# Row maxima split on VectorE before the turn, in an attention kernel that TensorE and VectorE share

## The chip, the cores and the metric

The kernel runs on one core of a Trainium2 chip. The metric is the device time of one execution in microseconds (us); of several runs the median counts. A profiled execution has a trace beside its time, and all durations below come from that one execution.

## The reference

Two branches with adaptive layer norm, one after the other, on `x` of 2048 rows by 512 columns: attention with 32 heads of 16 columns that share one key and one value head, and a bilinear gated feed-forward part with 1792 columns inside.

```
mod = (silu(c) @ w_mod).reshape(6, D)          # sa, ca, ga, sb, cb, gb
h = layernorm(x) * (1 + ca) + sa
q, k, v = h @ wq (32 heads x 16), h @ wk (16), h @ wv (16)
p = softmax(q k^T / 4)                         # per head, over 2048 keys
x = x + ga * ((p v) @ wo)
h = layernorm(x) * (1 + cb) + sb
x = x + gb * (((h @ w_gate) * (h @ w_up)) @ w_down)
```

## The kernel before

**Units.** The queries are cut into 4 blocks of 512 rows (`NB`), the 32 heads into 8 groups of 4 (`UB`); a block and a group make one of 32 units. Within a unit the keys go by in 16 tiles of 128 (`KT`). One step of the loop over key tiles is called a turn here: it makes four score products `sc` (L631, one for each head of the group, 128 keys by 512 queries), four exponentials on ScalarE (L633), and the four products `pv` of the turn before with the values (L642). So a unit has 16 turns, and `attend` writes two of them out at a time.

**Row maxima.** The exponentials need each query row's maximum over all keys, and it has to be there before a unit begins. Another set of score products `mx` (L581, 128 queries by 512 keys) therefore runs some 30 steps ahead, four in each turn; VectorE reduces each to one column of `mpart` (L584). When a unit's last `mx` has been reduced, `max_fin` (L601) takes the maximum over the four key blocks: `mm`, 128 rows by 16 columns. The maxima must then become rows of the operand `sst` of the next unit's score products: 48 of its 64 rows in each half hold the queries in f16 pieces, rows 48 and 49 (112 and 113 in the other half) the maximum, divided by 32, as a high and a low f16 part, so that the score product subtracts it by itself. `max_rows` does this. Its `f` turns `mm` on TensorE into a PSUM bank, `mxt` (L608). Its `g` writes the high part with a ScalarE copy (L613), the low part with a VectorE instruction that subtracts the high one (L614), both from PSUM into tiles `mt`, and sends each to `sst` with a DMA (L618) from SyncE's queue (SP).

**PSUM.** The eight banks (`NBANK`) are handed out from a queue: `ps_hold` takes the bank at its head, `ps_give` puts one back at its end, `ps_mx` and `ps_sc` do both at once. A TensorE product into a bank waits until the bank's last reader has finished. `pv` holds a bank for a whole unit, a side group holds one until it has ended.

**Side work.** Between the score products stand halves of side groups (L499): the q projection of later heads at first, then output projection and FFN of the block before. Each half uses 64 of TensorE's 128 rows, and a score product on the other 64 stands beside it. Three orders of a turn are written out by hand, `e` for a score product with its exponential, `m` for a maximum product, `x` for a half of a side group, the digit for the half of the rows:

```
NO_SIDE = "e0 e1 m0 m1 e0 e1 m0 m1"
FEW = "e1 m0 e0 x1 m0 x1 e0 x1 m0 x1 e1 m0"
MANY = "x1 e0 x1 m0 x1 e0 x1 e0 x1 m0 x1 m0 x1 m0 x1 e0"
```

FEW is for the q projection, MANY for output projection and FFN, NO_SIDE where no group is ready. In FEW and MANY the halves change roles in the second turn of each pair (`a ^ turn`).

**Order around the change.** `max_half` notes `f` and `g` in `later` when a unit's last maximum product has been issued, under the count of maximum steps from which they may run. `late_max` runs such an `f` and puts `g` into `posts`. It is called in the middle of a turn and behind the turn's `pv` products; `drain_posts` runs what is in `posts` at the start and in the middle of each turn, ahead of that half's products. `hooks` puts weight loads and other small steps between. With MANY and FEW two or more maximum products of the same half follow each other, and `f` comes to stand behind `pv` of the same turn in which the unit's last maximum product was made, `g` at the start of the next. The unit's last maximum product lies in its predecessor's turn 13 (counted from 0) with MANY and FEW, and at the end of turn 12 with NO_SIDE, where `f` then stands in the middle of turn 13. The new unit's first score products stand at the head of what would be turn 16.

Of the kernel before, what the change touches and what calls it, by code (L numbers as in the profile page):

```python
# [14 lines left out]
F16 = mybir.dt.float16  # L15
AF = mybir.ActivationFunctionType
OP = mybir.AluOpType
# [13 lines left out]
SPLIT_GAP = 2.5  # L31
NBANK = 8
QPRE = (20, 24)
TR_WAIT = 11
NHF = 12
V_STEP = 24
# [17 lines left out]
def adaln_mqa_glu_kernel(ctx: ExitStack, tc: tile.TileContext, x_in, wq_in, wk_in, wv_in, wo_in,  # L54
                         wg_in, wu_in, wd_in, c_in, wm_in, out):
    nc = tc.nc
# [5 lines left out]
    work = ctx.enter_context(tc.tile_pool(name="work", bufs=2))  # L62
# [7 lines left out]
    def ps_hold(name="side", shape=(128, 512)):  # L70

        tag, bufs = pool.popleft()
        t = psum.tile(list(shape), F32, name=name, tag=tag, bufs=bufs)
        held[id(t)] = (t, tag, bufs)
        return t

    def ps_give(t):
        _, tag, bufs = held.pop(id(t))
        pool.append((tag, bufs))
# [47 lines left out]
    ident = consts.tile([128, 128], F32, name="ident")  # L127
# [15 lines left out]
    identh = consts.tile([128, 128], F16, name="identh")  # L143
# [146 lines left out]
    for k in range(KC):  # L290
        for j in range(4):
            nc.tensor.matmul(pmA[32 * j:32 * j + 32, 0:256], silr[:, k, 0:32], wmA[:, k, 256 * j:256 * j + 256],
                             start=(k == 0), stop=(k == KC - 1))
# [248 lines left out]
    def load_q(u):  # L542
        b, g = divmod(u, UB)
        d = qd[b, g // 2].rearrange("(h e) l n -> e h l n", e=16)
        s = sst[u % 3]
        h0 = 4 * (g % 2)
        for a in range(2):
            for r, hl in ((0, 0), (1, 0), (2, 1)):
                nc.sync.dma_start(s[64 * a + 16 * r:64 * a + 16 * r + 16, :, :], d[:, h0 + a:h0 + a + 3:2, hl, :])
# [20 lines left out]
    def max_parts(u):  # L570
        if u < NU and u not in mparts:
            mparts[u] = work.tile([128, 2, 2, 4, 4], F32, name="mpart")
            if u == 0:
                nc.gpsimd.memset(mparts[u], LOW)

    def max_mm(u, a, op):
        kind, p, t, kc = op
        s = sst[u % 3]
        m = ps_sc() if kind == "diff" else ps_mx()
        keys = kdt[64 * a:64 * a + 48, :] if kind == "diff" else kst[64 * a:64 * a + 48, kc * 512:(kc + 1) * 512]  # L580
        nc.tensor.matmul(m, s[64 * a:64 * a + 48, p, t * 128:(t + 1) * 128], keys, start=True, stop=True)  # L581
        part = mparts[u][:, a, p, t, kc:kc + 1]
        if kind == "one":
            nc.vector.tensor_reduce(part, m, axis=AX.X, op=OP.max)  # L584
        elif kind == "diff":
            r = rel[a] = work.tile([128, 512], F32, name="rel", tag="gf", bufs=4)
            relus.append(lambda: nc.scalar.activation(r, m, AF.Relu))
        else:
            nc.vector.tensor_tensor_reduce(out=rel[a], in0=m, in1=rel[a], scale=1.0, scalar=LOW, op0=OP.add,
                                           op1=OP.max, accum_out=part)  # L590
# [6 lines left out]
    mms = {}  # L597
# [3 lines left out]
        nc.vector.tensor_reduce(mms[u], mparts[u].rearrange("p a q t k -> p a (q t) k"), axis=AX.X, op=OP.max)  # L601

    def max_rows(u):
        def f():
            mms[u, "b"] = ps_hold("mxt")
            p = mms[u, "b"][0:16, 0:128]
            mms[u, "p"] = p
            nc.tensor.transpose(p, mms[u].rearrange("p a c -> p (a c)"), ident)  # L608

        def g():  # L610
            p = mms[u, "p"]
            mt = [work.tile([16, 128], F16, name=f"mt{hl}") for hl in range(2)]
            nc.scalar.activation(mt[0], p, AF.Copy, scale=1.0 / 32.0)  # L613
            nc.vector.scalar_tensor_tensor(mt[1], p, 1.0 / 32.0, mt[0], op0=OP.mult, op1=OP.subtract)  # L614
            ps_give(mms[u, "b"])
            s = sst[u % 3]
            for hl in range(2):
                nc.sync.dma_start(s[48 + hl:113 + hl:64, :, :], mt[hl])  # L618
        return [(100, f, g)]

    pvb = {}
    ptl = {}
# [65 lines left out]
    def after(delay, f):  # L688
        if tick[0] is None:
            f()  # L690
        else:
            timers.setdefault(tick[0] + delay, []).append(f)
# [12 lines left out]
    def wo_work(b):  # L705
# [12 lines left out]
        def fin(t):  # L718
            def f(p):
# [28 lines left out]
                if t == 3:  # L748
                    for j, d in enumerate((2, 4, 6, 9) if b else (2, 4, 7, 12)):
                        after(d, n2f[b, j])  # L750
                    if b < NB - 1:
                        after(TR_WAIT if b else TR_WAIT + 3, lambda: turns.extend(ln2_work(b)))
            return f
# [7 lines left out]
    def ln2_work(b):  # L761
        items = []
        st = {}

        def tr(k):
            def f():
                if k == 0:
                    h2s[b] = big.tile([128, 2, KC, BT], F16, name="h2T", tag="wq")
                st["p"] = ps_hold("mx")
                for t in range(4):  # L770
                    nc.tensor.transpose(st["p"][:, t * 128:(t + 1) * 128], n2s[b, t][:, k * 128:(k + 1) * 128],  # L771
                                        ident)
            return f

        def ev(k):
            def f():
                hf = work.tile([128, BT], F32, name="hf", tag="g", bufs=2)
                nc.scalar.activation(hf, st["p"], AF.Identity, bias=hsc[:, k, 0:1], scale=hsc[:, k, 1:2])
                ps_give(st["p"])
                eng = nc.vector if b == NB - 1 else nc.gpsimd  # L780
                eng.tensor_scalar(h2s[b][:, 0, k, :], hf, 1.0, 0.0, op0=OP.mult, op1=OP.add)
                eng.tensor_tensor(h2s[b][:, 1, k, :], hf, h2s[b][:, 0, k, :], op=OP.subtract)
                if k == KC - 1:
                    h2done.add(b)
            return f

        for k in range(KC):
            items.append((900, tr(k), ev(k)))
        return items
# [248 lines left out]

    wlist, dlist, mod_rows = late_weights()
    NSTEP = 32  # L1040
    later = {}
    mstep = [0, 0]

    def drain_posts():
# [8 lines left out]
    def max_half(a):  # L1053
        n = mstep[a]
        mstep[a] += 1
        if n >= len(flat):
            return
        u, i, last, ops = flat[n]
        max_parts(u)
        for op in ops[a]:  # L1060
            max_mm(u, a, op)
        if a == 0:
            return
        if u + 1 < NU and i == QPRE[u > 0]:
            load_q(u + 1)
        if i == 12:
            max_parts(u + 1)
        if last:
            max_fin(u)
            (_, f, g), = max_rows(u)  # L1070
            later[mstep[1] + 1] = (f, g)

    def late_max():
        for at in [m for m in later if m <= mstep[1]]:
            f, g = later.pop(at)
            f()
            posts.append(g)
            return True
        return False


# [27 lines left out]
    for n in range(LEAD):  # L1109
# [9 lines left out]
        m, v = n - M_STEP, n - V_STEP  # L1119
# [30 lines left out]
    def attend(u, kt):  # L1150


        now[0] = u * NSTEP + 2 * kt
        if cur and cur[0].ended():
            cur.clear()
        side = None if u + kt == 0 else cur[0] if cur else fill[0][1] if open_gate(now[0]) else None
        style = NO_SIDE if side is None else FEW if side in qs else MANY
        order = [(w[0], int(w[1])) for w in style.split()]
        count = {}
        for turn in range(2):  # L1160
            now[0] = u * NSTEP + 2 * (kt + turn)
            sync["before"] = sync["exp"]
            drain_posts()
            for j, (what, a) in enumerate(order):
                if j == len(order) // 2:
                    drain_posts()
                    late_max()
                    hooks(u, 2 * (kt + turn))
                a = a if style is NO_SIDE else a ^ turn
                if what == "m" and mstep[a] >= len(flat) and style is MANY:  # L1170
                    mstep[a] += 1
                    side_half(a, second)
                elif what == "m":
                    max_half(a)
                elif what == "x":
                    side_half(a)
                else:
                    k = count[a] = count.get(a, -1) + 1
                    qk_exp(u, kt + (k // 2 if style is MANY else turn), k % 2, a)
            assert not sync["due"]  # L1180
            for g in ended:
                g.finish()
            ended.clear()
            for f in ends:
                f()
            ends.clear()
            v = u * KT + kt + turn - 1
            if v >= 0:
                pv(*divmod(v, KT))
                if v % KT == KT - 1:  # L1190
                    ends.append(lambda: pv_out(u - 1))
            if not late_max() and turns:
                _, f, post = turns.popleft()
                f()
                posts.append(post)
            hooks(u, 2 * (kt + turn) + 1)
# [19 lines left out]
    for u in range(NU):  # L1216
        if u == 1:
            side.extend(dlist)
        for kt in range(0, KT, 2):
            attend(u, kt)  # L1220
# [8 lines left out]
    u = NU - 1  # L1229
# [62 lines left out]
```

## Time and profile before

| | |
|---|---|
| median of 3 runs | 1699.75 us (1699.13 to 1699.99) |
| the profiled execution | 1698.53 us |
| its span, first to last instruction | 1696.5 us |
| mean granted TensorE clock | 0.996 |
| TensorE (PE) busy | 1653.9 us, 97% |
| VectorE (DVE) busy | 1392.2 us, 82% |
| ScalarE (ACT) busy | 1220.1 us, 72% |
| GpSimd (POOL) busy | 506.3 us, 30% |

The page lists the busy time of each engine, then groups of instructions by line (L), engine, operation and tile, with count, busy time, mean length in ns of one, and the engine's idle time just ahead of them with what ended it. A timeline has one row for each instruction or run of like instructions: start in us, length in us, engine, line, operation, what is written and read. PEld is TensorE's weight load, SPq SyncE's issue of DMAs.

### The profile page before, as it was taken

How to read it: one execution, taken by the hardware profiler on the slowest of the kernel's cores; microseconds unless marked ns; L12 is line 12 of the kernel's file. 1: busy time of each engine (PE TensorE's matmuls, PEld its weight loads, DVE VectorE, ACT ScalarE, POOL GpSimd, SP SyncE). 2: the span in 40 equal slices, each digit the busy share in tenths (PEclk: the TensorE clock that was granted, in tenths of full speed). 3: DMA queues.
4: the chain of work that ended last, by engine and by line, in shares of the span. 5: the costliest groups of instructions: out<-in, count | busy, mean ns of one | idle time of the engine just before them, and what ended most of it. 6: DMA issues, size and time to landing. Idle time of an engine off the chain costs nothing.

```text
span 1696.5 us, 33291 instructions
## 1 busy us (share of the span) xinstructions
PE 1653.9 (97%) x12709; PEld 535.1 (32%) x12709; DVE 1392.2 (82%) x2364; ACT 1220.1 (72%) x2295; POOL 506.3 (30%) x705
## 2 busy tenths in 40 slices
PE   6799999999999999999999999999999999999999
PEld 3223333222223333333333333333323333334444
DVE  7799999999998999999989999999998999703110
ACT  3678888888887787777787778787777787772010
POOL 5724445535676751110020110101011111112130
PEclk9899999999999999999999999999999999999999
DMA  5212222311322210001100000000010000001000
GB/s 203 99 36 84 64 79 66 96 35 56 83 81 59 67 41 9 17 9 29 34 5 18 16 16 9 16 10 16 17 39 11 22 15 9 12 4 42 19 1 25
DMA packets 48939, 66.64 MB, mean 39 GB/s; under 512 B 15302, under 2 KB 29450, under 8 KB 48780
## 3 DMA queue, kind: packets, MB, share of 16 engines
q1 hardware_dynamic: 47196, 64.33, 12.6%
q8 instruction: 99, 1.62, 0.4%
q14 instruction: 60, 0.49, 0.1%
q10 hardware_dynamic: 1584, 0.20, 0.1%
HBM read 51.12 MB, written 8.92 MB: 35 GB/s over the span
## 4 chain that ended last, share of the span: by engine, by line
PE 86%; DVE 7%; ACT 3%; POOL 1%; issue 1%; DMA 1%; SPq 0%; ACTq 0%; POOLq 0%
PE side L499 49%; PE pv L642 27%; DVE mpart L584 7%; PE sc L631 5%; PE mx L581 3%; ACT P L633 2%; DMA wmA<-in_w_mod_dram 1%; POOL h L415 1%; PE mx L771 1%; PE pk L257 0%; PE pq L352 0%; PE mxt L608 0%; ACT kwb L250 0%; DMA rc<-rs 0%; PE sc L247 0%
## 5 line engine op out<-in xcount | busy, mean ns | idle before, releaser
L584 DVE TENSOR_REDUCE mpart<-mx 128x1 f32<-128x512 f32 x2016 | 1267.1, 683 | 100.3 <-PE mx L581 95.3
L633 ACT ACTIVATE P<-sc 128x512 f32<-128x512 f32 x2048 | 1092.4, 599 | 263.0 <-PE sc L631 219.0
L631 PE MATMUL sc<-sst,kst 50*128 50x512 f16 x2048 | 664.4, 379 | 1.1 <-DVE mpart L584 0.6
L581 PE MATMUL mx<-kst,sst 48*128 48x512 f16 x2032 | 616.5, 377 | 11.6 <-DVE mpart L584 5.5
L642 PE MATMUL pv<-P,vst 128*32 128x512 f32 x4096 | 546.2, 605 | 1.2
L499 PE MATMUL side<-h2T,wg 64*128 64x512 f16 (+1 forms) x1168 | 284.3, 378 | 0.0
L499 PE MATMUL side<-h2T,wu 64*128 64x512 f16 (+1 forms) x1166 | 282.9, 378 | 0.1
L499 PE MATMUL side<-wd,glu 64*128 64x512 f16 (+1 forms) x1008 | 234.1, 378 | 2.2 <-ACT P L633 2.2
L824 POOL TENSOR_SCALAR glu<-gf 128x512 f16<-128x512 f32 x56 | 34.7, 620 | 633.8 <-DVE gf L823 552.9
L631 PEld LDWEIGHTS <-kst 50*128 50x128 f16 x2048 | 175.7, 94 | 130.9 <-issue 109.4
L581 PEld LDWEIGHTS <-sst 48*128 48x128 f16 x2048 | 182.3, 94 | 68.3 <-issue 44.3
L499 PEld LDWEIGHTS <-wg 64*128 64x128 f16 (+1 forms) x1168 | 100.8, 94 | 202.3 <-ACT P L633 94.8
L499 PEld LDWEIGHTS <-wu 64*128 64x128 f16 (+1 forms) x1166 | 100.7, 95 | 200.0 <-ACT P L633 92.4
L642 PEld LDWEIGHTS pv<-P,vst 128*32 128x32 f32 x4096 | 80.8, 108 | 216.1 <-issue 200.0
L499 PEld LDWEIGHTS <-glu 64*128 64x128 f16 (+1 forms) x1008 | 89.1, 95 | 165.5 <-ACT P L633 65.5
L823 DVE TENSOR_TENSOR gf<-side,g 128x512 f32<-128x512 f32 x56 | 38.3, 685 | 115.9 <-PE side L499 82.5
L499 PE MATMUL side<-h,wq 64*128 64x512 f16 (+1 forms) x372 | 98.3, 382 | 0.0
L818 ACT ACTIVATE g<-side 128x512 f32<-128x512 f32 x56 | 33.2, 593 | 81.5 <-PE side L499 81.5
L499 PE MATMUL side<-wo,och 64*128 64x512 f16 (+1 forms) x336 | 79.3, 378 | 0.0
L825 POOL TENSOR_TENSOR glu<-gf,glu 128x512 f16<-128x512 f32 x56 | 65.0, 1160 | 4.7
L190 POOL TENSOR_SCALAR rv<-st 128x1 f32<-128x1 f32 (+1 forms) x20 | 4.6, 228 | 169.3 <-DVE st L735 154.0
L912 POOL TENSOR_TENSOR kwb<-kwb,wsl 128x448 f32<-128x448 f32 (+1 forms) x40 | 47.6, 1189 | 3.1
(221 smaller groups left out, 770.9 us busy)
## 6 DMA issues: line engine op xcount, KB each, us to landing
wsl<-in_B_w_gate_dram SPq DMA_DIRECT2D x32, 224.0 KB
wsl<-in_B_w_up_dram SPq DMA_DIRECT2D x32, 224.0 KB
wsl<-in_B_w_down_dram SPq DMA_DIRECT2D x28, 256.0 KB
sst<-qd SPq DMA_DIRECT2D x186, 32.0 KB
qd<-q SPq DMA_DIRECT2D x16, 256.0 KB
oc<-ev SPq DMA_DIRECT2D x128, 32.0 KB
rr<-ri SPq DMA_DIRECT2D x16, 256.0 KB
xl<-in_A_x_dram SPq DMA_DIRECT2D x16, 256.0 KB
```

Source lines behind the costliest of these rows:

```text
L415: nc.gpsimd.tensor_tensor(lo, t, hi, op=OP.subtract)
L499: return nc.tensor.matmul(self.p, left[64 * r0:64 * r1], right[64 * r0:64 * r1], start=start, stop=self.ended())
L581: nc.tensor.matmul(m, s[64 * a:64 * a + 48, p, t * 128:(t + 1) * 128], keys, start=True, stop=True)
L584: nc.vector.tensor_reduce(part, m, axis=AX.X, op=OP.max)
L631: nc.tensor.matmul(t, kst[64 * a:64 * a + 50, kt * 128:(kt + 1) * 128], s[64 * a:64 * a + 50, p, :], start=True, stop=True)
L633: ex = nc.scalar.activation(ptl[u, kt, p, a], t, AF.Exp)
L642: nc.tensor.matmul(pvb[u][32 * j:32 * j + 32, :], vst[:, kt, :], ptl[u, kt, p, a], start=(kt == 0), stop=(kt == KT - 1))
L818: nc.scalar.activation(st["g", f], p, AF.Copy, scale=2.0 ** -45)
L823: nc.vector.tensor_tensor(gf, p, st["g", f], op=OP.mult)
L824: nc.gpsimd.tensor_scalar(st["glu"][:, 0, f, :], gf, 1.0, 0.0, op0=OP.mult, op1=OP.add)
L825: nc.gpsimd.tensor_tensor(st["glu"][:, 1, f, :], gf, st["glu"][:, 0, f, :], op=OP.subtract)
L912: nc.gpsimd.tensor_tensor(acc, acc, t, op=OP.add)
```

## The change

`max_rows` itself now issues two VectorE instructions right behind `max_fin`: they write the high f16 part of `mm`/32 and what is left of it into one tile `pk` of 128 rows by 32 columns, in SBUF. `f` turns `pk` with one f16 product against an f16 identity into a PSUM bank, where 32 rows come out. `g` copies the 32 rows to f16 with one ScalarE instruction and sends them with two DMAs, one for each half of the rows of `sst`; both parts of a half go in one DMA. The list `later` now counts calls: `late_max` is called behind `pv` alone, no longer in mid-turn; its first call behind the unit's last maximum product only counts down, the second runs `f`. So `f` stands behind the `pv` products of the turn after, and `g` at the start of the turn that follows.

```diff
+TURN_WAIT = 1
...
     def max_rows(u):
+        pk = work.tile([128, 2, 2, 8], F16, name="mmh")
+        nc.vector.tensor_scalar(pk[:, :, 0, :], mms[u], 1.0 / 32.0, None, op0=OP.mult)
+        nc.vector.scalar_tensor_tensor(pk[:, :, 1, :], mms[u], 1.0 / 32.0, pk[:, :, 0, :], op0=OP.mult,
+                                       op1=OP.subtract)
+
         def f():
             mms[u, "b"] = ps_hold("mxt")
-            p = mms[u, "b"][0:16, 0:128]
-            mms[u, "p"] = p
-            nc.tensor.transpose(p, mms[u].rearrange("p a c -> p (a c)"), ident)
+            nc.tensor.matmul(mms[u, "b"][0:32, 0:128], pk.rearrange("p a l c -> p (a l c)"), identh,
+                             start=True, stop=True)
 
         def g():
-            p = mms[u, "p"]
-            mt = [work.tile([16, 128], F16, name=f"mt{hl}") for hl in range(2)]
-            nc.scalar.activation(mt[0], p, AF.Copy, scale=1.0 / 32.0)
-            nc.vector.scalar_tensor_tensor(mt[1], p, 1.0 / 32.0, mt[0], op0=OP.mult, op1=OP.subtract)
+            mt = work.tile([32, 128], F16, name="mt")
+            nc.scalar.activation(mt, mms[u, "b"][0:32, 0:128], AF.Copy)
             ps_give(mms[u, "b"])
             s = sst[u % 3]
-            for hl in range(2):
-                nc.sync.dma_start(s[48 + hl:113 + hl:64, :, :], mt[hl])
-        return [(100, f, g)]
+            for a in range(2):
+                nc.sync.dma_start(s[64 * a + 48:64 * a + 50, :, :], mt[16 * a:16 * a + 16, :])
+        return f, g
...
-    later = {}
+    later = []
...
-            (_, f, g), = max_rows(u)
-            later[mstep[1] + 1] = (f, g)
+            later.append((TURN_WAIT, *max_rows(u)))
 
     def late_max():
-        for at in [m for m in later if m <= mstep[1]]:
-            f, g = later.pop(at)
+        if later and later[0][0] <= 0:
+            _, f, g = later.pop()
             f()
             posts.append(g)
             return True
+        later[:] = [(wait - 1, f, g) for wait, f, g in later]
         return False
...
                 if j == len(order) // 2:
                     drain_posts()
-                    late_max()
                     hooks(u, 2 * (kt + turn))
```

## The prediction

> **What bounds the kernel now.** I read the head of the page, its chain, the windows of three stretches, and then, engine by engine, the timeline around the one place in each unit that the change touches.
>
> ```profile
> span 1696.5 us, 33291 instructions
> ...
> PE 86%; DVE 7%; ACT 3%; POOL 1%; issue 1%; DMA 1%; SPq 0%; ACTq 0%; POOLq 0%
> ```
>
> ```profile
> 110.00:300.00 190.00, 189.04 (x1567) 60.55 (x1565) 186.19 (x318) 160.45 (x315) 87.57 (x90) 1.00 0.23 68
> 385.00:405.00 20.00, 18.43 (x134) 5.06 (x131) 19.93 (x38) 16.07 (x32) 13.18 (x22) 1.00 0.28 79
> 600.00:860.00 260.00, 259.42 (x2159) 79.77 (x2157) 240.97 (x397) 204.33 (x382) 44.00 (x65) 1.00 0.08 21
> ```
>
> ```profile
> L581 PE MATMUL mx<-kst,sst 48*128 48x512 f16 x2032 | 616.5, 377 | 11.6 <-DVE mpart L584 5.5
> ```
>
> TensorE is busy in nearly the whole span and the chain runs over it for 86%. The windows (columns: stretch, length, then PE, PEld, DVE, ACT, POOL) show that VectorE is no bystander. From 110 to 300 us, where the side work is the q projection, it has 186.19 of 190.00 us, and from 385 to 405, where there is none, 19.93 of 20.00: the row maxima set the pace there. From 600 to 860, with the FFN at the side, TensorE has 259.42 of 260.00 and VectorE 240.97. In the groups the score products for the maxima wait mostly for the maximum reductions (5.5 of 11.6 us): a PSUM bank comes back to TensorE only when its reader has finished. Of eight banks one is held by `pv` and one by the side group, six go round, and a bank is asked for again six allocations later. That hand-back is what I follow.
>
> **What is there today.** 31 units have their row maxima turned inside the attention loop, once in 16 turns. First VectorE, then TensorE, in one such unit of the FFN stage (start, length, engine, line):
>
> ```profile
> 1011.88 0.22 DVE L601 TENSOR_REDUCE mm<-mpart 128x16 f32<-128x64 f32 x1
> 1012.02 1.28 DVE L584 TENSOR_REDUCE mpart<-mx 128x1 f32<-128x512 f32 x2
> 1013.25 0.28 DVE L614 SCALAR_TENSOR_TENSOR mt<-mxt,mt 16x128 f16<-16x128 f32 x1
> 1013.49 2.54 DVE L584 TENSOR_REDUCE mpart<-mx 128x1 f32<-128x512 f32 x4
> 1016.33 0.69 DVE L584 TENSOR_REDUCE mpart<-mx 128x1 f32<-128x512 f32 x1 [0.30 <-PE mx L581]
> ```
>
> ```profile
> 1011.64 1.06 PE L642 MATMUL pv<-P,vst 128*32 128x512 f32 x8
> 1012.64 0.28 PE L608 MATMUL mxt<-ident,mm 128*16 128x128 f32 x1
> ...
> 1012.85 0.39 PE L631 MATMUL sc<-sst,kst 50*128 50x512 f16 x1
> ...
> 1013.08 0.38 PE L581 MATMUL mx<-kst,sst 48*128 48x512 f16 x1
> ...
> 1013.51 0.37 PE L631 MATMUL sc<-sst,kst 50*128 50x512 f16 x1
> ...
> 1013.73 0.38 PE L581 MATMUL mx<-kst,sst 48*128 48x512 f16 x1
> ...
> 1015.68 0.39 PE L631 MATMUL sc<-sst,kst 50*128 50x512 f16 x1
> ```
>
> On VectorE the final reduction `mm` starts at 1011.88, the next maximum reduction 0.14 later (1012.02), so `mm` costs 0.14. The split of the low half, L614, starts at 1013.25 and the next reduction at 1013.49: 0.24. With both, VectorE idles only at 1016.33, for 0.30, which is its slack in an ordinary turn. On TensorE the turned product `mxt` starts at 1012.64, 1.00 after `pv`, and the next turn at 1012.85: 0.21. So in this stage it stands behind the burst already; the change puts it one turn later. The next turn goes from 1012.85 to 1015.68, 2.83.
>
> **Part 1, the product.** The f32 turn of 0.21 becomes one f16 product of 128 columns. The nearest rows are four f32 turns at the same place, and an f16 product of 512 columns ahead of a score product:
>
> ```profile
> 498.94 0.66 PE L771 MATMUL mx<-ident,n 128*128 128x128 f32 x4
> 499.53 0.39 PE L631 MATMUL sc<-sst,kst 50*128 50x512 f16 x2
> ```
> and
> ```profile
> 85.12 0.38 PE L460 MATMUL pv<-h,wv 128*32 128x512 f16 x1 [1.84 <-POOL h L415]
> 85.43 0.39 PE L581 MATMUL mx<-kst,sst 48*128 48x512 f16 x2
> ```
>
> Four turns and the change to the next kind take 0.59 (498.94 to 499.53), one takes 0.21: 0.13 for each, 0.08 for the change of kind. The 512-column f16 product takes 0.31 (85.12 to 85.43), where such products follow each other at 0.22 (1013.51 to 1013.73): 0.09 for the change. So I price 128 columns at 0.22/4 + 0.09 = 0.15, between 0.05 (no change of kind) and 0.21 (no gain). Gain 0.06 a unit.
>
> **Part 2, the split.** Two VectorE instructions on 128x16 now stand right behind `mm`, each needing the one before. The trace has no such pair; nearest are two dependent small ones:
>
> ```profile
> 20.02 0.15 DVE L340 TENSOR_SCALAR kb<-kb 128x1 f32<-128x1 f32 x1
> 20.21 0.16 DVE L344 RECIPROCAL sck<-kb 128x1 f32<-128x1 f32 x1
> ```
>
> The second starts 0.04 after the first has ended. With 16 elements I take 0.16 and 0.17 for the rows' 0.15 and 0.16. A reduction starts 0.08 before its predecessor's end (1012.02 against 1011.88 + 0.22). From `mm` to the next reduction it is then 0.22 + 0.04 + 0.16 + 0.04 + 0.17 - 0.08 = 0.55 where it was 0.14: the reductions behind come **0.41 later**. Bounds: 0.14 if the two overlap like independent reductions (2 x 0.07), 0.64 if each is as long as L614 (2 x 0.28 + 2 x 0.04). I take 0.41, since both nearest rows are SBUF instructions of one engine in a chain. In the next turn the 0.24 of L614 goes; VectorE's net is +0.17 a unit.
>
> Queued behind the split are the last two reductions of the turn, and for them waits TensorE. In the unit shown they end at 1013.30 (1012.02 + 1.28); the second one's bank is asked for six allocations on: a score product, `mxt`, then 1012.85, 1013.08, 1013.29 and the product at 1013.51, 0.21 in hand. After the change `mxt` isn't in that turn, so TensorE is 0.21 earlier and the bank falls to the product now at 1013.73, then at 1013.52. The reduction ends at 1013.30 + 0.41 = 1013.71, with 0.04 of hand-over 1013.75: TensorE **waits 0.23**. The turn after starts at 1015.68 - 0.21 + 0.23 + 0.15 (the product behind it) = 1015.85: 0.17 lost. The wait is (delay - 0.18), so it decides. By the side work that the code puts beside them, 22 of the 31 units lie in this stage: **+3.7 us**.
>
> **The q-projection stage** has the first five units. Score and maximum products alternate there, and VectorE is nearly full (186.19 of 190.00):
>
> ```profile
> 165.43 0.22 DVE L601 TENSOR_REDUCE mm<-mpart 128x16 f32<-128x64 f32 x1
> 165.57 1.28 DVE L584 TENSOR_REDUCE mpart<-mx 128x1 f32<-128x512 f32 x2
> 166.77 0.28 DVE L614 SCALAR_TENSOR_TENSOR mt<-mxt,mt 16x128 f16<-16x128 f32 x1
> 166.97 3.17 DVE L584 TENSOR_REDUCE mpart<-mx 128x1 f32<-128x512 f32 x5
> ```
>
> ```profile
> 166.81 0.38 PE L581 MATMUL mx<-kst,sst 48*128 48x512 f16 x1
> ...
> 167.25 0.38 PE L581 MATMUL mx<-kst,sst 48*128 48x512 f16 x1
> ...
> 167.70 0.37 PE L581 MATMUL mx<-kst,sst 48*128 48x512 f16 x1
> ...
> 169.00 0.39 PE L631 MATMUL sc<-sst,kst 50*128 50x512 f16 x1
> ```
>
> Here the two late reductions end at 166.25 and 166.85 and serve, after the change, the products of 166.81 and 167.25, which come 0.21 earlier. First: 166.25 + 0.41 + 0.04 = 166.70 against 166.60, waits 0.10. Second: 167.30 against 167.25 - 0.21 + 0.10 = 167.14, waits 0.16. The next reduction starts at 167.26 - 0.08 and, 0.68 long, frees its bank at 167.90 for the product of 167.70, which is then at 167.75: 0.15. The turn after starts at 169.00 - 0.21 + 0.41 + 0.15 = 169.35: 0.35 lost, over five units **+1.8 us**.
>
> **The stage without side work** has the four others. Here `mxt` does stand in mid-turn:
>
> ```profile
> 327.11 0.39 PE L631 MATMUL sc<-sst,kst 50*128 50x512 f16 x2
> ...
> 329.51 0.39 PE L631 MATMUL sc<-sst,kst 50*128 50x512 f16 x2
> ...
> 330.64 0.27 PE L608 MATMUL mxt<-ident,mm 128*16 128x128 f32 x1 [0.52 <-ACT P L633]
> ...
> 332.37 0.39 PE L631 MATMUL sc<-sst,kst 50*128 50x512 f16 x2
> ```
>
> TensorE has idled 0.52 ahead of it, and this turn takes 2.86 (329.51 to 332.37) where the one before took 2.40. The change takes that wait out, but VectorE sets the pace there (19.93 of 20.00): what counts is its net +0.17, less what of the mid-turn wait was not VectorE's. Between -0.4 and +0.3 I take +0.1: **+0.4 us**.
>
> **Part 3, copy and rows.** One ScalarE copy of 32 rows for one of 16: both have 128 elements a row, nothing. The two DMAs have the same bytes, and now wait for ScalarE alone. But in the FFN and q stages they start a turn later (without side work the product only moves to the end of its turn, and the copy stays where it was), and must land before the next unit's first score product. They pass at most one weight load and one output store on SP's queue, which in this trace were ready when reached. In a unit of the q stage, from the start of the turn, and below it who waited for the DMAs of that line in the whole run:
>
> ```profile
> 166.36 0.39 PE L631 MATMUL sc<-sst,kst 50*128 50x512 f16 x1
> ...
> 166.47 0.27 ACT L613 ACTIVATE mt<-mxt 16x128 f16<-16x128 f32 x1 [0.33 <-PE mxt L608]
> ...
> 166.76 1.23 SPq L618 DMA_DIRECT2D sst<-mt  x2
> ```
>
> ```profile
>   PEld L631: 0.8, 1
> ```
>
> In before two turns lay between copy and use, twice 2.83 in the FFN stage, and one unit waited (0.8 us on the weight load). Now it is one turn: 2.83 there, 2.64 in the q-stage unit (166.36 to 169.00). The copy ends 0.38 into its turn (166.36 to 166.74), the second issue 1.63 into it (167.99), so 1.0 to 1.2 is left for landing. In the FFN stage the first turn of a unit reads only the half sent first, 0.6 earlier. I take no wait; for the range a landing of 1.5, 0.5 lost in each of the five q units, and 0.3 in each of the 22 if the score product waits for both halves.
>
> **Sum.** 3.7 + 1.8 + 0.4 = +5.9 us. The profiled execution took 1698.53 us (span 1696.5, 2.0 around it): 1704.5. The median of the runs, 1699.75, lies 1.2 above that execution, so the forecast on the runs' own scale is **1705.7 us**, 0.35% slower. Under 0.2% (3.4 us) a measurement of this kernel can't be told from no change.
>
> **Rivals.**
> *The split is cheap (chance 0.22).* If the two instructions delay the reductions by 0.24 or less, the wait in the FFN stage is at most 0.06 and that stage comes out at -0.06 to 0 a unit; the q-projection stage keeps some +0.1 to +0.2, the third -0.1 to +0.1: -1.3 to +1.3 us, so about 1699.7, no change. For it: VectorE has 0.30 idle in each turn of the long stage. Against it: small SBUF instructions take 0.15 and 0.16 here, in a chain, with 0.04 between. The Trainium skill, "VectorE: DVE Perf Modes", in the section on the TRN2 errata, gives an instruction from SBUF to SBUF 58 cycles plus its elements at 0.96 GHz, and about twice that fixed part from PSUM: an estimate of 0.08 us for each of the two, a delay of 0.24, and a sum of about +1.3 us. The same section says that the measured fixed part is nearer 150 cycles, and the 0.15 and 0.16 above agree with that one.
>
> *TensorE's stream decides (faster, 0.12).* Place: the product behind `pv`. If the split hides (delay under 0.18) and the product costs 0.05 because nothing switches, each FFN unit gains 0.16, 3.5 in all; the stage in mid-turn gets back 0.4 x 4 = 1.6; the q stage stays: -5.1, 1694.6 us. It decides from a product of under 0.10 on, with no wait on VectorE. For it: TensorE is 99.8% busy there. Against it: both f16 and f32 rows show the 0.08 to 0.09. The Trainium skill, "TensorE: Matmul & The Clock Gate", section "Back-to-back issue gap", gives 128 columns about 81 ns in a sustained stream; an estimate by it is 0.07 more gain a unit, some 2 us. No run here shows a lone f16 product of 128 columns.
>
> *The rows land late (0.10).* As the forecast, with 0.5 more in five units, 1708.2 us, and 0.3 more in 22, up to 1714.8; I take the middle, 1711. For it: half the time is left, and one unit waits already. Against it: 1.0 to 1.2 us for 4 KB, where the DMA share in the long stage is 0.08.
>
> **How the numbers follow.** The forecast has 0.56. The range goes from the cheap split's lower end, 1699.75 - 1.3 = 1698.5, to the middle of the late landing, 1711, which also holds a split of 0.6 in the FFN stage (22 x 0.36 = 7.9, and 2.5 from the others); what lies outside is the faster case and little else. The likeliest case's own range is 1703 to 1709. Slower: 0.56 + 0.10, less 0.04 for a forecast that comes out under the bound: 0.62. Same: 0.22 + 0.04 = 0.26. Faster: 0.12.
>
> **What would show it.** In the changed profile: a `mxt` with f16 in and 0.15 to the next product; two 128x16 instructions behind `mm` and 0.55 from `mm` to the next reduction; L614's group gone from VectorE; the wait of the maximum products for the reductions grown from 5.5 us to about 10; the turn with the maxima 0.2 shorter, the next one 0.35 to 0.4 longer; no score product waiting for `mt`. The forecast is wrong if the next turn in the FFN stage keeps its 2.83, or if `mm` to the next reduction is under 0.3, or if the first turn of a unit begins with a wait for the DMA.

## The result, and the profile after

| | before | after |
|---|---|---|
| median | 1699.26 us (6 runs, 1695.18 to 1699.99) | **1708.63 us** (6 runs, 1706.06 to 1712.64) |
| profiled execution, its span | 1698.53, 1696.5 us | 1706.06, 1703.9 us |
| mean granted TensorE clock | 0.996 | 0.998 |
| VectorE, GpSimd busy | 1392.2, 506.3 us | 1399.3, 506.2 us |

The ratio of after to before is 1.0061, with a 95% interval of [1.0049, 1.0074]: slower by 0.6%. The ratios below are given in the same way, each against runs of before made beside that kernel. The head of the changed kernel's page, its chain, and the two groups of score products (in a group: count, busy us, mean ns, then TensorE's idle time before them and what ended most of it):

```profile
span 1703.9 us, 33209 instructions
...
PE 81%; DVE 12%; ACT 2%; POOL 2%; DMA 2%; issue 1%; SPq 0%; ACTq 0%; POOLq 0%; DVEq 0%
...
L634 PE MATMUL sc<-sst,kst 50*128 50x512 f16 x2048 | 668.2, 378 | 4.8 <-DVE mpart L585 3.1
L582 PE MATMUL mx<-kst,sst 48*128 48x512 f16 x2032 | 616.3, 377 | 14.9 <-DVE mpart L585 7.5
```

VectorE's share of the chain rose from 7 to 12%, though its busy time rose by 7 us only: more often TensorE now waits for it. The FFN unit that the prediction showed, on VectorE, then on TensorE (of the pairs that start together only the attention's rows are shown):

```profile
1015.86 0.22 DVE L602 TENSOR_REDUCE mm<-mpart 128x16 f32<-128x64 f32 x1
1016.12 0.17 DVE L606 TENSOR_SCALAR mmh<-mm 128x16 f16<-128x16 f32 x1
1016.33 0.17 DVE L607 SCALAR_TENSOR_TENSOR mmh<-mm,mmh 128x16 f16<-128x16 f32 x1
1016.42 3.67 DVE L585 TENSOR_REDUCE mpart<-mx 128x1 f32<-128x512 f32 x6
```

```profile
1016.65 0.39 PE L634 MATMUL sc<-sst,kst 50*128 50x512 f16 x1
...
1017.32 0.37 PE L634 MATMUL sc<-sst,kst 50*128 50x512 f16 x1
...
1017.76 0.39 PE L582 MATMUL mx<-kst,sst 48*128 48x512 f16 x1
...
1018.87 1.06 PE L645 MATMUL pv<-P,vst 128*32 128x512 f32 x8
1019.75 0.22 PE L612 MATMUL mxt<-identh,mmh 128*32 128x128 f16 x1
...
1019.91 0.39 PE L634 MATMUL sc<-sst,kst 50*128 50x512 f16 x1
```

From `mm` to the next reduction 0.56 (before 0.14). The six reductions start 0.60 apart and last 0.68 each, so the second ends near 1016.42 + 0.60 + 0.68 = 1017.70, and the maximum product, due 0.22 after the score product at 1017.32, starts at 1017.76: a wait of 0.22. A later one waits 0.15 for the third. The turn takes 1019.91 - 1016.65 = 3.26 where it took 2.83. Note how little of this the groups show: of the 0.22 only 1017.76 - (1017.32 + 0.37) = 0.07 is idle time, since the product before, pipelined at 0.22, counts as busy for 0.37. A wait on TensorE is read here from starts, not from idle columns. Read in that way over all 22 units of the FFN stage, the starts in this turn that come late and lie some 0.05 behind the end of a VectorE instruction are late by 8.8 us in sum; before it was 0.8.

The same comparison over all units gives the table on which the rest stands: the sum over the units of a turn's length (first score product to first score product) less the same in before, in us. M is the turn of the maxima, M+1 and M+2 the next two.

| | 22 FFN units: M, M+1, M+2 | all turns | 5 q units: M, M+1, M+2 | all turns | 4 units without side work | tail |
|---|---|---|---|---|---|---|
| after | -3.83, +7.30, +0.41 | +4.8 | -1.45, +2.51, +1.18 | +2.0 | +1.6 | +1.7 |

Together +8.3 in the loop. "Tail" is what follows the last score product. Ahead of the first one, where the change does next to nothing, the profiled executions of the thirteen changed kernels differ from before by -2.7 to +4.4 us (here -2.7); the loop sums leave that out, the medians don't. Each sum compares two single executions, while runs of one kernel spread by 4 to 8 us, so the sums say where time is lost and the medians how much in all. Of the FFN units' +4.8, +3.9 lie in the three turns; where the other 0.9 come from stays open.

### The profile page after: what moved, and what is told of

The parts are those of the page before. It is cut to its first block, busy times and chain, and to the rows that moved or that the text cites. A ratio compares the mean times of both kernels' runs of the same rounds, so it can differ in the third digit from the quotient of the medians.

```text
span 1703.9 us, 33209 instructions
## 1 busy us (share of the span) xinstructions
PE 1657.6 (97%) x12701; PEld 535.1 (31%) x12701; DVE 1399.3 (82%) x2396; ACT 1222.0 (72%) x2295; POOL 506.2 (30%) x705
## 4 chain that ended last, share of the span: by engine, by line
PE 81%; DVE 12%; ACT 2%; POOL 2%; DMA 2%; issue 1%; SPq 0%; ACTq 0%; POOLq 0%; DVEq 0%
PE side L500 46%; PE pv L645 25%; DVE mpart L585 10%; PE sc L634 5%; PE mx L582 3%; ACT P L636 2%; POOL h L416 1%; DMA wmA<-in_w_mod_dram 1%; PE mx L774 1%; PE pk L258 0%; DMA rc<-rs 0%; PE pq L353 0%; SPq L659 0%; DMA sst<-mt 0%; DVE mmh L607 0%
## 5 line engine op out<-in xcount | busy, mean ns | idle before, releaser
L500 PE MATMUL side<-h2T,wg 64*128 64x512 f16 (+1 forms) x1166 | 282.6, 378 | 0.2
L500 PE MATMUL side<-h2T,wu 64*128 64x512 f16 (+1 forms) x1160 | 281.1, 378 | 0.1
L500 PE MATMUL side<-wd,glu 64*128 64x512 f16 (+1 forms) x1008 | 234.3, 378 | 2.3 <-ACT P L636 2.2
L500 PEld LDWEIGHTS <-wg 64*128 64x128 f16 (+1 forms) x1166 | 99.9, 94 | 206.9 <-ACT P L636 97.8
L500 PEld LDWEIGHTS <-wu 64*128 64x128 f16 (+1 forms) x1160 | 99.6, 95 | 201.0 <-ACT P L636 95.1
L500 PEld LDWEIGHTS <-glu 64*128 64x128 f16 (+1 forms) x1008 | 88.9, 95 | 167.7 <-ACT P L636 68.0
L500 PE MATMUL side<-h,wq 64*128 64x512 f16 (+1 forms) x372 | 98.3, 378 | 0.0
L500 PE MATMUL side<-wo,och 64*128 64x512 f16 (+1 forms) x336 | 80.1, 378 | 0.0
```

The source lines that it names most:

```text
L500: return nc.tensor.matmul(self.p, left[64 * r0:64 * r1], right[64 * r0:64 * r1], start=start, stop=self.ended())
```

## The experiments

Theories. **Hand-back** is the prediction's: the split stands ahead of the turn's last reductions, these return their banks later, and TensorE waits in M+1. **Lateness**: the product and the rows come a turn later, and that costs. **Port** came from the trace of after: there 12 of the 64 split instructions last not 0.175 us but 0.20 to 1.27. In one unit (VectorE, then GpSimd, same stretch):

```profile
593.53 0.22 DVE L602 TENSOR_REDUCE mm<-mpart 128x16 f32<-128x64 f32 x1
593.78 0.83 DVE L606 TENSOR_SCALAR mmh<-mm 128x16 f16<-128x16 f32 x1
594.65 0.54 DVE L607 SCALAR_TENSOR_TENSOR mmh<-mm,mmh 128x16 f16<-128x16 f32 x1
```
```profile
593.42 1.16 POOL L828 TENSOR_TENSOR glu<-gf,glu 128x512 f16<-128x512 f32 x1
594.56 0.62 POOL L1012 TENSOR_SCALAR wd<-wsl 128x512 f16<-128x512 f32 x1
```

L606 ends at 594.61, 0.03 after the GpSimd instruction that began before it, L607 at 595.19, 0.01 after the next one. So the third theory: a split instruction stands until such a GpSimd instruction is over.

### The split alone, and the rest alone

Before, with the two split instructions behind `max_fin` and their result unused:

```diff
     def max_rows(u):
+        pk = work.tile([128, 2, 2, 8], F16, name="mmh")
+        nc.vector.tensor_scalar(pk[:, :, 0, :], ...)
+        nc.vector.scalar_tensor_tensor(pk[:, :, 1, :], ...)
```

> The kernel before, with the two split instructions added behind the final reduction, their result unused; product, copy, low half and DMAs all as before. Hand-back: from mm to the next reduction 0.56 us instead of 0.14; in the FFN stage the bank asked for at 0.21 in hand comes 0.41 late, so the turn after the maxima is 0.2 to 0.4 longer than before in each of 22 units, the q stage 0.4 in five: +6 to +11 us, 1705 to 1710. Lateness: nothing moves in place, so 1699 to 1700. Port: some 4 us of the hand-back figure sit in the dozen units where a GpSimd instruction is running.

1710.28 us, 1.0067 [1.0053, 1.0081]: the two instructions alone cost as much as the whole change. M+1 of the FFN units grows by 9.06, M stays (-0.01). Here the low part's instruction of before stands in the next turn as well.

Before's f32 turn, copy and low part at the change's places (behind the next `pv`):

```diff
-        for at in [m for m in later if m <= mstep[1]]:
-            f, g = later.pop(at)
+        if later and later[0][0] <= 0:
+            _, f, g = later.pop()
...
-                    late_max()
```

> The turn and the split of before (f32 turn, high half on ScalarE, low half on VectorE from PSUM), called at the places of the change: product behind the burst of the next turn, copy and DMAs a turn later. Hand-back: VectorE has no more to do in front of the reductions, so about before: turn of the maxima 0.21 shorter, the next 0.21 longer, and the two DMAs late in the q stage by 0.4 to 0.6 in each of five units (the second waits for VectorE): 1699 to 1703. Lateness: the whole loss of the change, 1706 to 1710.

1702.13 us, 1.0019 [1.001, 1.0028]: the late places without the split cost some 3 of the 9 us. In the trace: +1.8 in the FFN units, +1.9 in the q units, -2.0 without side work, +1.8 in the tail.

### The product's place, and the split's

The change with the product a turn earlier, right behind the `pv` products (the burst) of the maxima's own turn:

```diff
-TURN_WAIT = 1
+TURN_WAIT = 0
```

> The changed kernel with the product one turn earlier, behind the burst of the turn of the maxima, copy and DMAs at the start of the next. Hand-back: the split stands where it was and the bank is asked for one allocation sooner, so the wait in the turn after is 0.25 to 0.35 in the FFN stage; the rows land in time in the q stage (-1.2): within 2.5 us of the change, 1706 to 1710. Lateness: back to before or under it, 1695 to 1700.

1717.54 us, 1.0113 [1.0096, 1.0129], outside both expectations, because the kernel got a wait of its own, on the split (who waited for `mmh`, us and times):

```profile
  PEld L612: 36.7, 32
...
  PE mxt L612: 11.7, 9
```

In the four units without side work this adds 8.9 us to the turn that ends with the unit's last maximum product; I hadn't seen that the product meets the unfinished split there. So the total decides nothing between the theories; the stages do. The FFN units' M+1 is +8.3 with the product a turn earlier, as hand-back has it, so lateness isn't the loss there. In the q units M+2 is 0.00 instead of +1.18, so that part was lateness.

The split in the middle of the next turn instead of behind `mm`:

```diff
-        nc.vector.tensor_scalar(pk[:, :, 0, :], ...)
+        def split():
+            nc.vector.tensor_scalar(pk[:, :, 0, :], ...)
...
+                    late_split()
```

> The changed kernel with the two split instructions issued in the middle of the next turn, no longer right behind the final reduction; the product, the copy and the DMAs stay where the change put them. Hand-back theory (the split delays the two reductions behind it, their banks come back late, TensorE waits in the next turn): the turn after the maxima falls from about 3.25 us back to 2.85 to 3.0 in the FFN stage, the turn of the maxima stays at 2.84, about 0.06 us a unit below before there; the q stage keeps VectorE's net 0.17 and its late rows. Whole: 1697 to 1702 us, -0.1% to +0.15% against before. Rival, lateness (product and copy one turn later are what costs): no better than the change, 1706 to 1711. Rival, port (the split waits for GpSimd wherever it stands): stretched instructions again in about 10 units, 1700 to 1704.

1704.3 us, 1.0033 [1.0021, 1.0044]. In M+1 the FFN units lose 0.25 instead of 7.30: that part of hand-back is shown. The total misses the 1697 to 1702 expected, for the tail's +1.7 and for +3.05 in the FFN units' M+2. That is mostly the hand-back one turn on: the split now stands ahead of reductions whose banks are asked for there, and starts some 0.05 behind the end of a VectorE instruction are late by 3.5 us in sum (before 0.7). The product behind the turn waits for the split as well, but of its own four waits only one, of 0.5 us, is in an FFN unit (who waited for `mmh`):

```profile
  PEld L614: 11.0, 10
  PE mxt L614: 3.2, 4
```

### How much delay, how much loss

One split instruction on VectorE, the low half of the maxima left out and filled with zeros by GpSimd:

```diff
-        nc.vector.scalar_tensor_tensor(pk[:, :, 1, :], mms[u], 1.0 / 32.0, pk[:, :, 0, :], ...)
+        nc.gpsimd.memset(pk[:, :, 1, :], 0.0)
```

> The changed kernel with one VectorE instruction behind the final reduction instead of two: the low half is filled with zeros by GpSimd, so the low half of the maxima is left out. Hand-back theory (the loss in the next turn is the delay of the reductions less about 0.18 us): mm to the next reduction falls from 0.56 to about 0.35, the delay from 0.41 to 0.21, the wait in the next turn to 0.03; the turn after the maxima in the 22 FFN units loses 0 to 3 us in sum instead of 7.3, and the whole takes 1700 to 1704 us. If the loss doesn't go with the delay but with the product's new place, the sum stays at about 7 and the whole at 1706 to 1709 us. If the port theory carries most of the loss, the one instruction is still stretched in about a third of the units and the sum falls by no more than half.

1702.87 us, 1.0029 [1.0019, 1.0038], as hand-back has it; M+1 of the FFN units +3.4, a little over the 0 to 3 expected, of which six units with a stretched split bring 1.7; the units without side work are at -1.3. Loop and tail of the profiled execution come to +2.0 where the medians differ by 5.0; where the rest lies stays open. And the reverse, the change with a useless GpSimd product of 128x512, 1.04 us long, started beside the split:

```diff
+        junk = work.tile([128, 16, 32], F16, name="junk", bufs=1)
+        mb = mms[u].rearrange("p a c -> p (a c)")[:, :, None].to_broadcast([128, 16, 32])
+        nc.gpsimd.tensor_tensor(junk, mb, mb, op=OP.mult)
```

> The changed kernel with one more GpSimd instruction, a 128x512 product of the maxima with themselves that nothing reads, issued behind the final reduction, so that it starts beside the first VectorE instruction of the split in each of the 31 units. Port theory (a VectorE instruction from SBUF to SBUF stands still until a GpSimd instruction that started before it has ended): the second instruction of the split is stretched from 0.18 us to the rest of the GpSimd instruction's length in nearly all units, mm to the next reduction grows from 0.56 to 1.0 or more, the turn after the maxima loses another 0.4 or more per unit, and the profiled execution takes 1718 us or more. If the stretched instructions beside GpSimd's were a coincidence, mm to the next reduction stays at 0.56 in most units and the time at 1706 to 1711 us.

1729.01 us (one execution, span 1727.0; 23 over after's profiled execution). Its split instructions (shortest/median/longest in ns), and its chain:

```profile
L609 DVE TENSOR_SCALAR mmh<-mm x32: 174/175/737, 75.4 to 1506.9; 128x16 f16<-128x16 f32 x32
L610 DVE SCALAR_TENSOR_TENSOR mmh<-mm,mmh x32: 489/905/970, 75.6 to 1507.1; 128x16 f16<-128x16 f32 x32
```
```profile
PE 73%; DVE 21%; ACT 2%; POOL 2%; DMA 1%; issue 1%; SPq 0%; DVEq 0%; ACTq 0%; POOLq 0%
```

In 26 of 32 the GpSimd instruction starts just after L609 has begun, and L609 keeps its 175 ns; L610, behind it, is stretched in all 32, 30 times beside this instruction and twice beside another of GpSimd's, and ends 0.02 to 0.03 after it. So a split instruction that starts behind a running GpSimd instruction stands until that one has ended, and the order of starts decides; why is not in the trace. With the split off VectorE (below), the four kernels give one line, in the FFN units:

| | `mm` to next reduction, usual | M+1 per unit |
|---|---|---|
| split on GpSimd | 0.14 | +0.02 |
| one instruction | 0.34 to 0.41 | +0.15 |
| the change | 0.56 | +0.33 |
| the change, stretched in every unit | 1.29 | +1.02 |

From the second row on, each 0.1 us by which the reductions come later costs TensorE about 0.1. The means of M+1 hold stretched units too. In the units without a stretched split (in the last row, those where only the added GpSimd instruction stretches it) they are +0.11, +0.28 and +1.03 in the last three rows, at 0.38, 0.56 and 1.30 from `mm` to the next reduction. Less 0.035 for the product (below), that is a wait of the delay less 0.16 to 0.18, and the prediction had 0.18.

### The tail

`late_max` returning true also keeps a turned layer-norm group from its place. In the last unit without side work the kernel before turned such a group at 498.94 (the first L771 row in the prediction); now the product stands in that turn, and the first group comes at 503.4:

```profile
L774 PE MATMUL mx<-ident,n x64: 272/273/330, 503.4 to 1569.4; 128*128 128x128 f32 x64
```

The gate, the condition under which FFN groups may begin, opens a turn later, and products that had room in the loop are left for the tail. Products at L499/L500 behind the last score product, before and then after:

```profile
L499 PE MATMUL side<-h2T,wg 128*128 128x512 f16 (+1 forms) x181 | 41.8, 379 | 0.0
L499 PE MATMUL side<-h2T,wu 128*128 128x512 f16 (+1 forms) x180 | 41.5, 379 | 0.0
```
```profile
L500 PE MATMUL side<-h2T,wu 128*128 128x512 f16 (+1 forms) x189 | 43.7, 379 | 0.0
L500 PE MATMUL side<-h2T,wg 128*128 128x512 f16 (+1 forms) x180 | 41.5, 379 | 0.0
```

Eight more at 0.22: 1.76 us, and the tail is 1.73 longer. Taking the coupling out, first alone in the change:

```diff
-            if not late_max() and turns:
+            late_max()
+            if turns:
```

> The changed kernel, but the call that turns the maxima behind the burst no longer keeps one of the layer norm's turns from going out in the same place (the change does so in one unit that has no side work at that moment, which opens the FFN's gate a turn later). Shifted side work: 16 half products of the FFN go back from the tail into the loop, and the stretch behind the last score product is 1.7 us shorter than the change's 169.5: 1.5 to 2.5 us below the change, 1706 to 1707.5. If instead the longer tail has another cause: no difference, 1708 to 1710.

1710.54 us, 1.0066 [1.0054, 1.0079]: a miss, not told apart from the change. The tail is back (+0.01), but the FFN units' M+1 grew to +8.81 and the whole loop by 0.95; why, stays open. With the split in mid-turn the same edit:

> The split in mid-turn and the freed turns together. Hand-back plus shifted side work: both add up, 1701.5 to 1703.5, +0.1% to +0.25%; what is left over before are the rows that land late (T15 of the q stage, about 1.5 us) and waits of TensorE for a split that stands behind a late reduction. If the split's place and the tail have a common cause: no better than the split in mid-turn alone, 1704 to 1705.

1702.29 us, 1.0016 [1.0007, 1.0025] against 1.0033 without it. In the traces of the two kernels with the split in mid-turn the loop is the same (+2.07 and +2.05) and the tail shorter by 1.72. So the coupling is shown to make the tail longer; whether the whole gains by taking it out depends on the kernel: not in the change itself, by the tail's whole 1.7 us where the split is out of the way.

### The split on GpSimd, and the mid-turn call

```diff
-        nc.vector.tensor_scalar(pk[:, :, 0, :], ...)
-        nc.vector.scalar_tensor_tensor(pk[:, :, 1, :], ...)
+        ms = work.tile([128, 2, 8], F32, name="mms")
+        nc.gpsimd.tensor_scalar(ms, mms[u], 1.0 / 32.0, 0.0, ...)
+        nc.gpsimd.tensor_scalar(pk[:, :, 0, :], ms, 1.0, 0.0, ...)
+        nc.gpsimd.tensor_tensor(pk[:, :, 1, :], ms, pk[:, :, 0, :], ...)
```

> The changed kernel with the split as three small GpSimd instructions in place of two on VectorE. Hand-back: VectorE has nothing but mm there, so the turn after the maxima loses its 7 us in the FFN stage, and VectorE's 0.24 of the low half is gone: 1698 to 1703 (the tail's 1.7 and the late rows stay), if the product one turn later finds the split ready. Port or queue on GpSimd: in the first dozen units, where GpSimd is working on weights, the product waits 1 to 3 us for it: 1705 to 1715. Lateness: as the change, 1706 to 1711.

1702.3 us, 1.0013 [1.0004, 1.0022]. The loop is now 1.7 us shorter than before's: -0.8 in the FFN units, -1.7 without side work, +0.85 in the q units. With the layer-norm group freed as well:

> The kernel with the split on GpSimd, and now the product of the maxima no longer keeps a turned layer-norm group from its place (the group may go in the same turn). The loop sum with the split on GpSimd was 1.7 us under the kernel before and the tail 1.73 us over it; without the tail's part: 1697 to 1700 us. If freeing the group costs in the loop what it saves in the tail, as it did beside the VectorE split, 1701 to 1703 us.

1699.2 us, 1.0002 [0.9994, 1.0011]: no difference from before, tail +0.02, loop -1.9. The q units still lose in M+2 (+1.4), where the rows land late: score products waited 4.3 + 1.0 us for `mt`. So for the first five units before's f32 turn, one burst behind the maxima, and the rest as above:

```diff
-            later.append((TURN_WAIT, *max_rows(u)))
+            if u < QUNITS:
+                later.append((0 if u else TURN_WAIT, *max_rows_ps(u)))
+            else:
+                later.append((TURN_WAIT, *max_rows(u)))
```

> The split on GpSimd and the freed layer-norm groups for the units from the sixth on, and in the first five, whose side work is the q projection, the kernel before's f32 turn one burst after the maxima. It takes the landing of the rows one turn later out of those five units, where the split on GpSimd lost 0.85 us in sum. If the late rows are that loss: 1696 to 1699 us, at or under the kernel before without its mid-turn call (1696.5); if not, the same as the split on GpSimd with freed groups within 1 us.

1695.46 us against 1697.88 for before beside it, **0.9983** [0.9971, 0.9994]; loop -4.2 (FFN -2.1, q -0.6, no side work -1.4), tail +0.01. Its GpSimd split (the second and third of three instructions) and who waited for `mt`:

```profile
L609 POOL TENSOR_SCALAR mmh<-mms x26: 204/204/207, 331.5 to 1475.5; 128x16 f16<-128x16 f32 x26
L610 POOL TENSOR_TENSOR mmh<-mms,mmh x26: 218/219/221, 331.8 to 1475.8; 128x16 f16<-128x16 f32 x26
```
```profile
  PEld L654: 0.8, 1
  PE sc L654: 0.2, 1
```

Last, before itself without its mid-turn call, and with the group freed; nothing else of the change:

```diff
-                    late_max()
...
-            if not late_max() and turns:
+            late_max()
+            if turns:
```

> The kernel before with its product never in mid-turn: the mid-turn call is left out and the call behind the burst doesn't hold up a layer norm turn. Only the four units without side work change: their product moves to the end of its turn, f32, split, copy and DMAs as before. From the late-place run these four units took 2.0 us less: 1696.5 to 1698, -0.08% to -0.15%. If the mid-turn wait is VectorE's in any case: 1699 to 1700.

1696.45 us against 1699.74 for before beside it, 0.9985 [0.9976, 0.9994]. It too beats both kernels, with two small edits to the order of calls. The profiled execution doesn't show all of it (loop -0.85, of it -1.0 in the units without side work; its time, 1698.86, is among the longest of its eleven): where the rest of the 3.3 us lies stays open. The two best are not told apart.

## Why the prediction was right, and where its terms were not

Forecast 1705.7, measured 1708.63, inside the range and on the side that had 0.62. The mechanism was the forecast one; several sizes were not, and part of the agreement is errors that cancel.

- **The product.** From `mxt` to the next turn 0.15 was forecast and 0.152 measured in nearly all units, and yet the price was wrong. It isn't the time to the next product that counts but what the product adds from `pv` to the next turn. Without it that is 1.00 (in before 1015.68 - 1014.68, with the row below; also the median over the FFN stage). With the f32 turn it was 1.21, with the f16 product it is 1.04 (above, 1019.91 - 1018.87), because `mxt` starts 0.88 after `pv`, 0.12 sooner than a score product does. So the product costs 0.035 where 0.15 was put in, and its gain is 0.17 a unit, not 0.06: most of what I charged to it as a change of kind is in the 1.00 that is there without it. Whether the type or the 32 columns, as many as `pv` has, brings that was not tried.

```profile
1014.68 1.06 PE L642 MATMUL pv<-P,vst 128*32 128x512 f32 x8
```

- **The split.** 0.55 from `mm` to the next reduction forecast, 0.56 measured where nothing disturbs it. Its lengths are 0.175, as the chain of small SBUF instructions at 20 us suggested. The cheap split (0.22) is refuted.
- **The hand-back in the FFN stage.** The product that waits is the one named, for 0.22 where 0.23 was said; the second wait in that turn was not foreseen, and other units wait less. In the mean of the 15 units with an undisturbed split M+1 grows by 0.28, of which 0.035 is the product and 0.24 the waits; M shrinks by 0.18. Such a unit costs +0.10, not +0.17: the product was priced 0.115 too high, and against that M shrank by 0.03 less than the 0.21 forecast. The stage's M to M+2 come to +3.9 us against +3.7 all the same: what fills the sum up is the next point. That the two agree so well is luck. The rival "TensorE's stream decides" was thus right about the product and wrong about the split. With the split on GpSimd (freed groups) M and M+1 come to -3.98 + 0.47 = -3.5 us, 0.16 a unit, which is the gain it named.
- **Overlooked: GpSimd.** The bounds of the split (0.14 to 0.64) took its neighbours on VectorE only. In 9 of 31 units a stretched split makes it 0.68 to 1.66. Six of these are FFN units; of that stage's +7.3 in M+1 they bring 3.1, 0.52 each, and the 15 undisturbed ones 4.1. Three of the four units without side work are among the nine too (0.82 to 1.66). That stage was to cost +0.4 and cost +1.6; with the split on GpSimd it gains 0.8 to 1.7 us. That the stretched splits make its cost is not shown: unit by unit the three come to +0.9, +0.4 and -0.3, and the undisturbed one to +0.5.
- **The q stage.** +1.8 forecast, +2.0 measured, by other parts: hand-back +0.21 a unit (-1.45 + 2.51 over five) instead of 0.35, and then +1.18 in M+2 for rows that land late, which I had taken as nothing. Two issues of the DMA on SP's queue, now 0.64 each (before 0.54), and the turn lost were enough:

```profile
L621 SPq DMA_DIRECT2D sst<-mt x64: 610/642/709, 79.2 to 1488.2; - x64
...
  PEld L634: 4.0, 5
  PE sc L634: 0.8, 2
```

 The rival "the rows land late" was therefore no alternative to the forecast but an addition to it, at half its price in those five units and none in the other 22 (+0.4 in M+2). "No score product waiting for `mt`" was wrong, and with it one of the prediction's own signs of being wrong came true: the first turn of these five units begins with a wait for the DMA, 0.2 to 1.3 us on the weight load (in before one unit, 0.8).
- **Overlooked: the tail**, +1.7 us. The diff shows it only to a reader who asks what else hangs on the value that `late_max` returns.
- **The sign to look for.** The maximum products' wait for reductions was to go from 5.5 to about 10 us; it is 7.5, with 3.1 at the score products (before 0.6). The waits are there, but the column counts only what exceeds the pipelined product ahead.

Sum: +8.3 in the loop and +1.7 behind it, 10.0 against the 5.9 forecast. The medians of the runs differ by 9.4.

## What to carry to other kernels

Work put into an engine's queue ahead of the instructions that return buffers cost its full length here as soon as the buffers' slack was used up, even where that engine had idle time in every turn; try it on an engine that nobody waits for. Price a small VectorE instruction with what GpSimd runs at that moment, and a small product by what it adds between its neighbours, not by the gap behind it. Where a step moves, follow the value it returns and the transfers it issues: here one kept other work from its place, the other had a turn less to land.

## What the runs showed of the hardware

An f16 product of 128 columns between `pv` and a score product adds 0.035 us, an f32 turn of the same columns at the same place 0.207.

A VectorE instruction of 16 elements a row, SBUF to SBUF, takes 0.175 us, but up to 1.27 us when a GpSimd instruction is running as it starts: it ends 0.02 to 0.03 us after the other in nearly all cases. In the kernel with the forced collision none of the 26 split instructions that began first was stretched, and of the 38 that began while a GpSimd instruction was running 37 were; for the last, the GpSimd instruction ended 0.09 us after its start. The 128x512 reductions from PSUM kept their length: 0.681 in the median of the 166 that lay within a GpSimd instruction in after, and of the 1249 that touched none. The Trainium skill, "SBUF — State Buffer", section "Who interferes with whom", bears on this: VectorE and GpSimd share a pair of ports, an exclusive lock, and whoever issues first holds it for the whole instruction while the other is blocked. A VectorE instruction with two SBUF inputs contends for it with a GpSimd instruction that reads SBUF, `tensor_scalar` can do so in its 2-port modes where its operands allow them, and on trn2 a `tensor_reduce` never does. This case's traces agree in who was held up, for how long, and in the reductions' 0.681; the ports themselves no trace shows. The prediction didn't weigh that section; it would have spoken against the split's upper bound of 0.64.
